# Channel attention and two feed-forward layers on one core: weights in separate tiles, one lag of five, all of layer 2 by Strassen steps, an own order for the end

## The chip, the cores and the metric

One core of a Trainium2 chip runs the whole program. The metric is the device time of one execution in microseconds (us). The kernel before took 1023.1 to 1024.99 us in three runs, with a median of 1024.78 us. The core's engines are PE (matrix products), DVE (vector), ACT (scalar and activation functions), POOL (a second elementwise engine) and SP (which issues the transfers). Each works through its own queue in order.

## The reference

All arrays are float32. There are 6016 tokens, 256 channels and a hidden width of 2048.

```python
qn = q / (np.linalg.norm(q, axis=1, keepdims=True) + 1e-06)     # over the tokens
kn = k / (np.linalg.norm(k, axis=1, keepdims=True) + 1e-06)
s = kn.transpose(0, 2, 1) @ qn / tau                            # 256 x 256
a = softmax(s)                                                  # over the last axis
x = (v @ a)                                                     # 6016 x 256
h = x @ moe_w_in;  x = (h - np.tanh(h)) @ moe_w_out             # 256 -> 2048 -> 256
h = x @ moe2_w_in
g = np.where(h > 0.0, h, np.exp(np.minimum(h, 0.0)) - 1.0)
out = g @ moe2_w_out
```

## The kernel before

**Values in two parts.** A float32 matrix is held as a high part (rounded to what PE multiplies in one pass) and a low part (the rest). A product is three matmuls: high by high, high weights by low values, low weights by high values. `win` and `wout` hold one layer's two weight matrices, high and low part in one tile each.

**Blocks and steps.** After the attention (whose 256 by 256 matrix is folded into layer 1's first weights) the tokens are worked in 12 blocks, 11 of 512 tokens and a last, narrow one of 384. A step (layer, block b, slice p of 0 to 7) makes 256 of the 2048 hidden values for one block: the first products, the activation, the split of the result into `ghi` (ACT, L917) and `glo` (POOL, L920), and 12 matmuls that add its share to the two output sums `o0` and `o1` (PSUM, L1018). The code counts layers from 0: `(0, 11, p)` is layer 1's narrow block and `(1, 0, p)` the first block of layer 2.

**Plain and Strassen steps.** A plain step's first products are 12 matmuls with 512 columns (384 in the narrow block). A Strassen step (`Step.one` to `Step.seventh`) makes seven products of half blocks, 21 matmuls with 256 columns, from sums of the weights (`ws`, loaded from DRAM for every step into three buffers, L666) and of the values (`thi`, `tlo`). Its chain `qa` is read three times on the way by ACT (`copies`, L860); DVE joins the pieces (`merge` L864, `close` L870, `close_chain` L875). In layer 2 before, `strassen` is true for the 512-wide blocks except for slice 5 (`PLAIN`). The sums for layer 2 are made on POOL while layer 1 runs (`sums_of`).

**What sets the order.** Nothing schedules: each engine works in the order in which the code issues. From layer 1's narrow block to the end one loop over `i` (L1235) issues one step per turn and, between its pieces, work of earlier steps: the activation of step i-2, its end and split of step i-3 (`three`; in layer 1 all of it with step i-2), and the output products of an old step. That is step i-4 in layer 1 and step i-5 in layer 2, so that the turn i = 12 has none; turns 0, 1 and 3 carry those of layer 1's last 512-wide block. When an old step has p = 7, its block's sums are complete: `emit_evac` moves `o0` by ACT at the end of the turn and `o1` at the beginning of the next turn (`behind`; ACT in layer 1 except in its last block, otherwise DVE). The next turn's old step has p = 0 and starts the same two sums again (a boundary, `boundary`). In layer 2 this turn is always a step with p = 5. Within a Strassen turn the last two products of the step before (`tail.four`, `tail.three`, issued by `finish`) come after six output products and after `six` and `five`.

**The transition.** While layer 1's narrow block runs, the turns issue on SP the loads of layer 2's weights: `win` slice p after step (0, 11, p) has used the old one (L1386), `wout` slice p after the output products of (0, 11, p) (L1372), 512 KB each, and `ws` two steps ahead.

**The end.** After the last step five turns with no new step remain (`cur is None`). They finish the activations of the last three steps and issue the output products of the last five. `exp` of a step goes into one PSUM tile (`ps_b`, one buffer), so that it waits for the `end` of the step before.

Of the kernel before, what the change touches and what calls it, by code (L numbers as in the profile page):

```python
# [8 lines left out]
F32 = mybir.dt.float32  # L9
# [13 lines left out]
def kernel(  # L23
# [40 lines left out]
    win_hi, win_lo = win[:, 0], win[:, 1]  # L64
    wout_hi, wout_lo = wout[:, 0], wout[:, 1]

    PAIRS = (1, 3, 5, 7)
    PLAIN = (5,)

# [455 lines left out]
    with tc.manual_schedule():  # L525
# [271 lines left out]
        class Step:  # L797
# [87 lines left out]
                else:  # L885
                    nc.vector.tensor_copy(out=self.h[:, 1], in_=q)

            def exp(self):
                self.e = ps_b.tile([P, 2, 512], F32, tag="o", name=f"e{self.name}")[:, :, : self.n]
                nc.scalar.activation(out=self.e, in_=self.h, func=AF.Exp)  # L890

            def tanh(self):
# [339 lines left out]

        halves_of_unit = []
        behind = []
        for i in range(len(todo) + LAG):  # L1235
            cur = None
            if i < len(todo) and todo[i] == (1, 0, 0):
                assert conv.done() and not conv.ready and not sums_left
            if i < len(todo):
                layer, b, p = todo[i]  # L1240
                cur = Step(layer, b, p, sums_at.pop(i, None))
                steps.append(cur)
                if p == 0 and nv < len(phases):
                    load_v(nv)
                    raw_of[0] = v_of[nv]
            prv, two, three = at(i - 1), at(i - 2), at(i - 3)
            tail = prv if prv and prv.seven else None
            old = at(i - 4) if at(i - 4) and at(i - 4).layer == 0 else at(i - 5)
            if old and old.layer == 0 and old is not at(i - 4):
                old = None  # L1250
            parts, done = [], None
            if old:
                done = (old.layer, old.b, old.p)
                parts = out_products(*done, (old.hi, old.lo), last=(i == len(todo) + LAG - 1))
            elif i in early_outs:
                done = early_outs[i][:3]
                parts = out_products(*early_outs[i])
# [4 lines left out]
                    part()  # L1262
                del parts[:n]

            before_act, after_act, scalar_mid, scalar_end, pool_end = [], [], [], [], []
            if cur and nv < len(phases):
# [12 lines left out]
            if cur and layer == 0:  # L1279
# [4 lines left out]
            first = two if two and two.layer == 0 else None  # L1284
            second = two if two and two.layer == 1 else None
            third = three if three and three.layer == 1 else None

            def vector_begin():
                if tail and boundary:
                    tail.merge()  # L1290
                while behind:
                    emit_evac(*behind.pop(), (1,))
                if third:
                    third.end()
                if tail and not boundary:
                    tail.merge()
                for f in before_act:
                    f()
                if first:
                    first.begin()  # L1300

            def finish():
                if tail:
# [7 lines left out]
            def act_b():  # L1311
                if i == 0:
                    before.upper()
                    before.lower()
                if first:
# [6 lines left out]
            if cur is None:  # L1322
                if two:
                    two.tanh()
                vector_begin()
                out(6)
                finish()
            elif cur.seven:
# [6 lines left out]
                out(6)  # L1335
                cur.six()
                cur.copy(2)
                cur.five()
                finish()
            else:  # L1340
                cur.plain(0)
                cur.plain_copy(0)
# [6 lines left out]
                else:  # L1349
                    out(6)  # L1350
                    finish()
            if cur:
                fetch_sums(i + 2)
            act_b()
            if cur is None:
                out(12)
            elif cur.seven:
                out(3)
                cur.seventh()
                cur.copy(1)  # L1360
# [3 lines left out]
                cur.plain_copy(1)  # L1364
                out(12)
            if done:
                last_block = i >= len(todo)
                emit_evac(*done, range(KC) if last_block else (0,))
                if done[2] == NP - 1 and not last_block:
                    behind.append(done)  # L1370
                if done[:2] == (0, NBLK - 1):
                    nc.sync.dma_start(  # L1372
                        out=wout[:, :, 2 * done[2] : 2 * done[2] + 2].bitcast(F32), in_=out_dram2[done[2]]
                    )
            for f in scalar_mid:
                f()
            if third:
                third.upper()
                third.lower(nc.vector if cur is None else None)
            for f in scalar_end:  # L1380
                f()
            for f in pool_end:
                f()
            if cur and (layer, b) == (0, NBLK - 1):
                fs = slice(2 * P * p, 2 * P * (p + 1))
                nc.sync.dma_start(  # L1386
                    out=win[:, :, :, fs].bitcast(F32), in_=in_dram[p].rearrange("p k d i f -> p k d (i f)")
                )
            if cur and p == NP - 1:
                nv += 1  # L1390


# [33 lines left out]
```

## Time and profile before

| | us |
|---|---|
| median of three runs | 1024.78 |
| the profiled execution | 1024.82 |
| its span, first to last instruction | 1023.0 |
| PE busy in the span | 1009.8 |
| DVE, ACT, POOL busy | 816.5, 742.5, 488.2 |

The profile is of one execution. A matmul's busy time is modelled: in a stream one with 512 columns starts about 0.216 us after the last and is shown as 0.38 us long, so starts tell more than lengths. A wait is idle time of an engine, with the instruction whose end released it. The granted clock is a share of 2.4 GHz; 0.5 is 1.2 GHz.

### The profile page before, as it was taken

What the parts mean: (1) busy time and instruction counts of PE and PEld (TensorE: products, weight loads), DVE (VectorE), ACT (ScalarE), POOL (GpSimd) and SP (SyncE); (2) the same over time, 40 slices, a digit from 0 to 9 for tenths busy, and PEclk for the clock granted to TensorE, in tenths of its full rate; (3) what the DMA queues carried; (4) which work ended last, traced back from release to release, by engine and by line L of the source; (5) the groups of instructions that cost most, each with busy time, mean ns of one, the idle gap of its engine ahead of it and who ended that gap; (6) DMA issues with size and microseconds to landing.
All of it is one profiled execution on the core that took longest, in us unless ns stands there. A gap on an engine that the chain in (4) does not pass through costs nothing.

```text
span 1023.0 us, 15755 instructions
## 1 busy us (share of the span) xinstructions
PE 1009.8 (99%) x5935; PEld 922.9 (90%) x5935; DVE 816.5 (80%) x1068; ACT 742.5 (73%) x1086; POOL 488.2 (48%) x309
## 2 busy tenths in 40 slices
PE   9999999999999999999989999999999999999998
PEld 8888888899999999898989999999999999999997
DVE  7899988899999999999536777777777777777765
ACT  7877775656656666576457888888888888888765
POOL 4522210243434342344445676676676666766542
PEclk9999999999999999999999999999999999999999
DMA  9832120232222232221258333433333433333200
GB/s 351 297 103 83 42 93 31 73 103 93 94 72 83 94 112 90 67 94 58 83 185 315 113 104 124 140 108 125 124 124 105 130 135 106 114 119 113 83 9 28
DMA packets 61468, 115.58 MB, mean 113 GB/s; under 512 B 4944, under 2 KB 26704, under 8 KB 61392
## 3 DMA queue, kind: packets, MB, share of 16 engines
q1 hardware_dynamic: 61104, 114.05, 33.1%
q8 instruction: 47, 0.77, 0.3%
q10 hardware_dynamic: 288, 0.52, 0.1%
q14 instruction: 29, 0.24, 0.1%
HBM read 90.18 MB, written 24.38 MB: 112 GB/s over the span
## 4 chain that ended last, share of the span: by engine, by line
PE 95%; DVE 3%; ACT 2%; issue 1%; DVEq 0%; ACTq 0%
PE o L1018 45%; PE h L283 13%; PE qa L830 10%; PE qb L830 7%; PE S L351 4%; PE qb L283 3%; PE qa L283 3%; PE q L756 2%; PE q L755 2%; PE q L754 2%; PE aw L283 1%; PE o_last L1018 1%; DVE g L955 0%; PE warm L363 0%; ACT ghi L917 0%
## 5 line engine op out<-in xcount | busy, mean ns | idle before, releaser
L1018 PE MATMUL o<-ghi,wout 128*128 128x512 f32 (+1 forms) x1472 | 362.3, 378 | 2.7 <-ACT osb L1046 2.7
L920 POOL TENSOR_TENSOR glo<-g,ghi 128x1024 fp32r<-128x1024 f32 (+1 forms) x101 | 233.7, 2314 | 179.8 <-ACT ghi L917 177.1
L1018 PEld LDWEIGHTS o<-ghi,wout 128*128 128x128 f32 x1472 | 262.6, 190 | 29.7 <-ACT osb L1046 3.2
L1018 PE MATMUL o<-glo,wout 128*128 128x512 f32 (+1 forms) x736 | 199.7, 377 | 0.0
L795 POOL TENSOR_TENSOR glo<-g,ghi 128x1024 fp32r<-128x1024 f32 x32 | 76.4, 2386 | 196.7 <-ACT ghi L791 152.0
L902 DVE SCALAR_TENSOR_TENSOR e<-e,g 128x1024 f32<-128x1024 f32 (+1 forms) x96 | 115.8, 1206 | 54.5 <-ACT e L890 54.5
L1018 PEld LDWEIGHTS o<-glo,wout 128*128 128x128 f32 x736 | 133.0, 190 | 15.0
L860 ACT ACTIVATE copies<-qa 128x256 f32<-128x256 f32 x231 | 88.2, 382 | 72.7 <-PE qa L830 72.4
L283 PE MATMUL h<-vhi,win 128*128 128x512 f32 x424 | 134.8, 379 | 0.7 <-DVE g L955 0.7
L910 DVE SCALAR_TENSOR_TENSOR g<-e,hs 128x1024 f32<-128x1024 f32 (+1 forms) x96 | 115.1, 1199 | 6.9 <-DVE e L902 0.5
L917 ACT ACTIVATE ghi<-g 128x1024 fp32r<-128x1024 f32 (+1 forms) x104 | 106.1, 1020 | 7.8 <-DVE g L906 5.4
L895 ACT ACTIVATE g<-hs 128x1024 f32<-128x1024 f32 (+1 forms) x96 | 99.8, 1040 | 0.0
L890 ACT ACTIVATE e<-hs 128x1024 f32<-128x1024 f32 (+1 forms) x96 | 96.9, 1010 | 2.1 <-DVE g L910 2.1
L283 PEld LDWEIGHTS h<-vhi,win 128*128 128x128 f32 x424 | 80.1, 189 | 12.5 <-ACT wout L203 1.1
L783 ACT ACTIVATE g<-hs 128x1024 f32<-128x1024 f32 x32 | 33.9, 1059 | 78.4 <-DVE hs L773 78.4
L791 ACT ACTIVATE ghi<-g 128x1024 fp32r<-128x1024 f32 x64 | 67.6, 1057 | 22.0 <-DVE g L788 22.0
L875 DVE COPY hs<-qa 128x256 f32<-128x256 f32 x77 | 32.5, 423 | 63.9 <-PE qa L830 63.9
L283 PE MATMUL h<-vlo,win 128*128 128x512 f32 x212 | 80.3, 379 | 0.0
L830 PE MATMUL qa<-thi,ws 128*128 128x256 f32 x308 | 76.5, 274 | 1.2 <-ACT copies L860 1.2
L162 DVE CUSTOM_DVE_ANT_0 cut<-cut,low 128x512 uint16<-128x512 uint16 (+1 forms) x48 | 64.6, 1345 | 0.5
L830 PEld LDWEIGHTS qa<-thi,ws 128*128 128x128 f32 x308 | 58.7, 190 | 5.5 <-ACT copies L860 1.4
L864 DVE TENSOR_TENSOR hs<-qb,copies 128x512 f32<-128x512 f32 x77 | 52.4, 680 | 2.0 <-ACT copies L860 2.0
(209 smaller groups left out, 2305.3 us busy)
## 6 DMA issues: line engine op xcount, KB each, us to landing
ws<-sums SPq DMA_DIRECT2D x77, 512.0 KB, 3.3
qk<-in_q_dram SPq DMA_DIRECT2D x23, 256.0 KB, 5.1
vraw<-in_vT_dram SPq DMA_DIRECT2D x11, 512.0 KB, 4.0
x<-osb SPq DMA_DIRECT2D x22, 256.0 KB, 2.0
vraw<-x SPq DMA_DIRECT2D x11, 512.0 KB, 4.3
out_dram<-osb SPq DMA_DIRECT2D x22, 256.0 KB, 2.0
qk<-in_k_dram SPq DMA_DIRECT2D x21, 256.0 KB, 5.2
raw0in<-in_moe_w_in_dram SPq DMA_DIRECT2D x8, 512.0 KB, 3.6
```

The source lines that it names most:

```text
L283: nc.tensor.matmul(out=out, lhsT=w, rhs=x, start=(i == 0), stop=(i == len(pairs) - 1))
L791: nc.scalar.activation(out=self.hi, in_=self.g, func=AF.Copy)
L795: engine.tensor_tensor(out=self.lo, in0=self.g, in1=self.hi.bitcast(F32), op=ALU.subtract)
L830: nc.tensor.matmul(out=out, lhsT=w, rhs=x, start=start and k == 0, stop=k == 2, skip_group_check=True,)
L860: nc.scalar.activation(out=self.copies[:, k], in_=self.qa[:, :W], func=AF.Copy)
L890: nc.scalar.activation(out=self.e, in_=self.h, func=AF.Exp)
L895: nc.scalar.activation(out=self.g, in_=self.h, func=AF.Tanh, scale=0.5)
L902: nc.vector.scalar_tensor_tensor(out=self.e, in0=self.e, scalar=1.0, in1=self.g, op0=ALU.add, op1=ALU.mult)
L910: nc.vector.scalar_tensor_tensor(out=self.g, in0=self.e, scalar=0.0, in1=self.h, op0=ALU.min, op1=ALU.max)
L917: nc.scalar.activation(out=self.hi, in_=self.g, func=AF.Copy)
L920: (engine or nc.gpsimd).tensor_tensor(out=self.lo, in0=self.g, in1=self.hi.bitcast(F32), op=ALU.subtract)
L1018: nc.tensor.matmul(out=columns(o[c][:, :n]), lhsT=w[:, f, c * P : (c + 1) * P], rhs=turned(x[:, i]), start=(f == 0 and w is wout_hi and x ...
```

## The change

1. `win` and `wout` become two tiles each, for the high and the low parts, and each load of layer 2's weights becomes two of 256 KB.
2. `PLAIN` is empty: slice 5 of layer 2's 512-wide blocks becomes a Strassen step too. Its weight sums are made, stored and loaded like the others'. At a boundary a Strassen turn calls `finish` before the six output products.
3. The old step is i-5 in both layers. Layer 1's narrow block splits its activation with step i-3, and turn 12 has output products while turn 4 has none. `o1` of layer 1's last 512-wide block is moved by DVE.
4. The five turns at the end are replaced by a straight list for the last three steps x, y and z; z's `exp` gets a PSUM tile of its own.

```diff
-    win = wpool.tile([P, 2, KC, F], F32R, name="win")
-    wout = wpool.tile([P, 2, F // P, C], F32R, name="wout")
...
+    win_hi, win_lo = win = [wpool.tile([P, KC, F], F32R, name=f"win_{k}") for k in ("hi", "lo")]
+    wout_hi, wout_lo = wout = [wpool.tile([P, F // P, C], F32R, name=f"wout_{k}") for k in ("hi", "lo")]
...
-    PLAIN = (5,)
+    PLAIN = ()
...
-                if c and (layer or b == NBLK - 1):
+                if c and (layer or b >= NBLK - 2):
                     nc.vector.tensor_copy(out=to, in_=of)
...
-            old = at(i - 4) if at(i - 4) and at(i - 4).layer == 0 else at(i - 5)
-            if old and old.layer == 0 and old is not at(i - 4):
-                old = None
+            old = at(i - LAG)
...
-                if first:
-                    first.upper()
-                    first.lower()
-                if second:
-                    second.exp()
-                    second.begin()
+                if two:
+                    two.exp()
+                    two.begin()
...
-                out(6)
-                cur.six()
-                cur.copy(2)
-                cur.five()
-                finish()
+                if boundary:
+                    finish()
+                    out(6)
+                    cur.six()
+                    cur.copy(2)
+                    cur.five()
+                else:
+                    out(6)
+                    cur.six()
+                    cur.copy(2)
+                    cur.five()
+                    finish()
...
+                for k in range(2):
+                    nc.sync.dma_start(
+                        out=win[k][:, :, fs].bitcast(F32), in_=in_dram[p][:, k].rearrange("p d i f -> p d (i f)")
+                    )
...
+        x, y, z = steps[-3:]
+        emit_rest(steps[-5])
+        y.tanh()
+        x.end()
+        x.upper()
+        x.lower()
+        y.exp()
+        y.begin()
+        z.tanh()
+        z.exp(ps_e)
+        emit_rest(steps[-4])
+        y.end()
+        z.begin()
+        y.upper()
+        y.lower()
+        z.end()
+        z.upper()
+        z.lower(nc.vector)
+        emit_rest(x)
+        emit_rest(y)
+        emit_rest(z, last=True)
+        emit_evac(z.layer, z.b, z.p)
```

PE in layer 1's narrow block, before: `qa_11_4` and `qb_11_4` are the two halves of step (0, 11, 4), and `o_0_11` are the two sums of this block.

```order
2392 L283 MATMUL qa_11_4_5282<-vlo_4962,win 128x384
2395 L283 MATMUL qa_11_4_5282<-vhi_4909,win 128x384 x2
2396 L1018 MATMUL o_0_11_5284<-ghi,wout 128x384
2397 L1018 MATMUL o_0_11_5285<-ghi,wout 128x384
2402 L283 MATMUL qb_11_4_5283<-vhi_4909,win 128x384
2406 L283 MATMUL qb_11_4_5283<-vhi_4909,win 128x384 x2
2413 L283 MATMUL qa_11_5_5326<-vhi_4909,win 128x384
```

The same place now:

```order
2492 L281 MATMUL qa_11_4_5293<-vhi_4920,win_hi 128x384
2494 L281 MATMUL qa_11_4_5293<-vhi_4920,win_lo 128x384 x2
2495 L281 MATMUL qb_11_4_5294<-vhi_4920,win_hi 128x384
2499 L281 MATMUL qb_11_4_5294<-vhi_4920,win_lo 128x384 x2
2500 L281 MATMUL qa_11_5_5323<-vhi_4920,win_hi 128x384
2504 L281 MATMUL qa_11_5_5323<-vhi_4920,win_lo 128x384 x2
2505 L1018 MATMUL o_0_11_5325<-ghi,wout_hi 128x384
2506 L1018 MATMUL o_0_11_5326<-ghi,wout_hi 128x384
```

The first output product of the narrow block has moved from the middle of step 4 to the middle of step 5, behind the second half of step 4 and the first of step 5.

PE at a boundary of layer 2, before: the end of turn (1, 1, 4), then turn (1, 1, 5); `o_1_0` are the sums of block 0, `o_1_1` those of block 1.

```order
2878 L1018 MATMUL o_1_0_5724<-glo,wout 128x512
2879 L283 MATMUL qa_1_5_6167<-vhi_5556,win 128x512
2880 L283 MATMUL qa_1_5_6167<-vlo_5558,win 128x512
2881 L283 MATMUL qa_1_5_6167<-vhi_5556,win 128x512
2882 L283 MATMUL qa_1_5_6167<-vlo_5558,win 128x512
2883 L283 MATMUL qa_1_5_6167<-vhi_5556,win 128x512 x2
2884 L830 MATMUL qa_1_4_6105<-thi_5717,win 128x256
2889 L830 MATMUL qb_1_4_6106<-vhi_5556,ws_6030 128x256
```

The same place now:

```order
2988 L1018 MATMUL o_1_0_5751<-glo,wout_hi 128x512
2989 L828 MATMUL qa_1_5_6212<-vhi_5563,win_hi 128x256
2991 L828 MATMUL qa_1_5_6212<-vhi_5563,win_lo 128x256
2992 L828 MATMUL qb_1_5_6213<-vhi_5563,win_hi 128x256
2994 L828 MATMUL qb_1_5_6213<-vhi_5563,win_lo 128x256
2995 L828 MATMUL qa_1_4_6150<-thi_5743,win_hi 128x256
3000 L828 MATMUL qb_1_4_6151<-vhi_5563,ws_6073 128x256
3001 L1018 MATMUL o_1_1_6215<-ghi,wout_hi 128x512
```

Between the last product of the old sums and the first of the new stand 12 matmuls with 256 columns; before, there were six with 512 columns and six with 256.

ACT in the last stretch, before, from the `hs` of the last step on (`g` is `tanh`, `e_11_6` and `e_11_7` the `exp` of the last two steps, `ghi` the split):

```order
1054 L884 ACTIVATE hs<-qa_11_7_10650 128x384
1055 L895 ACTIVATE g<-hs 128x2x384
1056 L890 ACTIVATE e_11_5_10669<-hs 128x2x384
1057 L917 ACTIVATE ghi<-g 128x2x384
1058 L895 ACTIVATE g<-hs 128x2x384
1059 L890 ACTIVATE e_11_6_10698<-hs 128x2x384
1060 L917 ACTIVATE ghi<-g 128x2x384
1061 L895 ACTIVATE g<-hs 128x2x384
1062 L890 ACTIVATE e_11_7_10720<-hs 128x2x384
1063 L917 ACTIVATE ghi<-g 128x2x384 x2
```

The same stretch now:

```order
1074 L882 ACTIVATE hs<-qa_11_7_10853 128x384
1075 L895 ACTIVATE g<-hs 128x2x384
1076 L890 ACTIVATE e_11_5_10872<-hs 128x2x384
1077 L917 ACTIVATE ghi<-g 128x2x384
1078 L895 ACTIVATE g<-hs 128x2x384
1079 L917 ACTIVATE ghi<-g 128x2x384
1080 L890 ACTIVATE e_11_6_10915<-hs 128x2x384
1081 L895 ACTIVATE g<-hs 128x2x384
1082 L890 ACTIVATE e_11_7_10920<-hs 128x2x384
1083 L917 ACTIVATE ghi<-g 128x2x384 x2
```

The split of step x stands before the `exp` of step y instead of behind it.

## Rows read from the trace of the kernel before

**Rows 1.** Windows, from:to, length, busy by engine, PE clock, DMA share, GB/s.

```profile
510.00:560.00 50.00, 46.10 (x292) 44.58 (x292) 23.91 (x36) 32.38 (x53) 24.48 (x16) 0.97 0.67 235
600.00:975.00 375.00, 375.00 (x2402) 347.65 (x2401) 278.05 (x368) 310.86 (x480) 247.33 (x138) 1.00 0.35 117
975.00:1023.00 48.00, 43.01 (x242) 40.21 (x240) 27.59 (x35) 27.67 (x39) 16.66 (x9) 1.00 0.05 20
```

**Rows 2.** Waits of PE: who waited for whom, us in total, times, longest.

```profile
PE o L1018 <- ACT osb L1046: 2.7, 2, 1.5
PE o_last L1018 <- ACT ghi L917: 1.5, 2, 0.8
PE qa L830 <- ACT copies L860: 1.2, 1, 1.2
PE qb L830 <- DVE hs L864: 0.3, 1, 0.3
```

**Rows 3.** Timeline, narrow block: start, us, engine, instruction, idle before.

```profile
518.09 0.33 PE L283 MATMUL qa<-vhi,win 128*128 128x384 f32 x1
...
519.28 1.01 ACT L1046 ACTIVATE osb<-o 128x512 f32<-128x512 f32 x1
...
522.31 1.79 PE L1018 MATMUL o<-ghi,wout 128*128 128x384 f32 x5 [1.54 <-ACT osb L1046]
...
526.86 0.33 PE L283 MATMUL qa<-vhi,win 128*128 128x384 f32 x1
...
530.76 0.33 PE L283 MATMUL qa<-vhi,win 128*128 128x384 f32 x1
```

**Rows 4.** Windows, PE alone: length, PE busy, granted clock, DMA.

```profile
521.00:524.00 3.00, 1.69 (x6) 0.76 0.80 261
```

**Rows 5.** Chain of waits, in order of time: first six output products of three turns.

```profile
595.41 1.30 PE o L1018 x6
...
610.46 1.30 PE o L1018 x6
615.39 1.30 PE o L1018 x6
```

**Rows 6.** Timeline, all engines, boundary turn (1, 1, 5).

```profile
599.51 0.38 PE L283 MATMUL qa<-vhi,win 128*128 128x512 f32 x1
599.55 0.68 DVE L864 TENSOR_TENSOR hs<-qb,copies 128x512 f32<-128x512 f32 x1
...
600.15 0.68 DVE L1044 COPY osb<-o 128x512 f32<-128x512 f32 x1
...
600.75 1.21 DVE L910 SCALAR_TENSOR_TENSOR g<-e,hs 128x1024 f32<-128x1024 f32 x1
600.80 0.27 PE L830 MATMUL qa<-thi,win 128*128 128x256 f32 x1
...
601.47 1.46 PE L1018 MATMUL o<-ghi,wout 128*128 128x512 f32 x6
```

**Rows 7.** Windows, start of layer 2.

```profile
535.00:555.00 20.00, 20.00 (x148) 19.80 (x148) 10.40 (x16) 14.68 (x27) 11.05 (x7) 1.00 0.95 353
```

**Rows 8.** DMA, window 540.55:541: issue, count, KB each, us to landing.

```profile
ws<-sums SPq DMA_DIRECT2D x1, 512.0 KB, 7.5
```

**Rows 9.** Timeline, PE: the first product that reads these sums.

```profile
548.22 0.35 PE L830 MATMUL qa<-thi,ws 128*128 128x256 f32 x1
```

**Rows 10.** Timeline, all engines, the end of the program.

```profile
1007.29 1.46 PE L1018 MATMUL o_last<-ghi,wout 128*128 128x384 f32 x8
1007.39 1.83 POOL L920 TENSOR_TENSOR glo<-g,ghi 128x768 fp32r<-128x768 f32 x1 [2.08 <-ACT ghi L917]
...
1007.92 0.95 DVE L910 SCALAR_TENSOR_TENSOR g<-e,hs 128x768 f32<-128x768 f32 x1
1008.90 0.81 ACT L890 ACTIVATE e<-hs 128x768 f32<-128x768 f32 x1 [0.86 <-DVE g L910]
...
1019.07 0.49 PE L1018 MATMUL o_last<-glo,wout 128*128 128x384 f32 x2
```

More of the change, by code (lines that the diff above doesn't have):

```diff
@@ L886, in plain_copy, with exp @@
                     nc.vector.tensor_copy(out=self.h[:, 1], in_=q)
-            def exp(self):
-                self.e = ps_b.tile([P, 2, 512], F32, tag="o", name=f"e{self.name}")[:, :, : self.n]
+            def exp(self, pool=None):
+                if self.layer == 0:
+                    return
+                self.e = (pool or ps_b).tile([P, 2, 512], F32, tag="o", name=f"e{self.name}")[:, :, : self.n]
                 nc.scalar.activation(out=self.e, in_=self.h, func=AF.Exp)
@@ L1234 @@
         behind = []
-        for i in range(len(todo) + LAG):
-            cur = None
-            if i < len(todo) and todo[i] == (1, 0, 0):
+        for i in range(len(todo)):
+            layer, b, p = todo[i]
+            if todo[i] == (1, 0, 0):
                 assert conv.done() and not conv.ready and not sums_left
[L1239 to L1245, printed above, removed]
+            cur = Step(layer, b, p, sums_at.pop(i, None))
+            steps.append(cur)
+            if p == 0 and nv < len(phases):
+                load_v(nv)
+                raw_of[0] = v_of[nv]
             prv, two, three = at(i - 1), at(i - 2), at(i - 3)
             tail = prv if prv and prv.seven else None
-            old = at(i - 4) if at(i - 4) and at(i - 4).layer == 0 else at(i - 5)
-            if old and old.layer == 0 and old is not at(i - 4):
-                old = None
+            old = at(i - LAG)
             parts, done = [], None
@@ L1253 @@
                 done = (old.layer, old.b, old.p)
-                parts = out_products(*done, (old.hi, old.lo), last=(i == len(todo) + LAG - 1))
+                parts = out_products(*done, (old.hi, old.lo))
             elif i in early_outs:
@@ L1278 @@
                     pool_end.append(lambda: half_of_sums_lower(nv, p - 5))
-            if cur and layer == 0:
+            if layer == 0:
                 vector, scalar, pool = conversion(i)
@@ L1283 @@
                 pool_end += pool
-            first = two if two and two.layer == 0 else None
-            second = two if two and two.layer == 1 else None
-            third = three if three and three.layer == 1 else None
             def vector_begin():
@@ L1292, in vector_begin @@
                     emit_evac(*behind.pop(), (1,))
-                if third:
-                    third.end()
+                if three:
+                    three.end()
                 if tail and not boundary:
@@ L1314, in act_b @@
                     before.lower()
[L1315 to L1328 removed]
+                if two:
+                    two.exp()
+                    two.begin()
+            if cur.seven:
                 cur.one()
@@ L1351 @@
                     finish()
-            if cur:
-                fetch_sums(i + 2)
+            fetch_sums(i + 2)
             act_b()
-            if cur is None:
-                out(12)
-            elif cur.seven:
+            if cur.seven:
                 out(3)
@@ L1366 @@
             if done:
-                last_block = i >= len(todo)
-                emit_evac(*done, range(KC) if last_block else (0,))
-                if done[2] == NP - 1 and not last_block:
+                emit_evac(*done, (0,))
+                if done[2] == NP - 1:
                     behind.append(done)
                 if done[:2] == (0, NBLK - 1):
[L1372 to L1379, printed above, removed]
+                    for k in range(2):
+                        nc.sync.dma_start(
+                            out=wout[k][:, 2 * done[2] : 2 * done[2] + 2].bitcast(F32),
+                            in_=out_dram2[done[2]][:, k],
+                        )
+            if three:
+                three.upper()
+                three.lower()
             for f in scalar_end:
@@ L1383, with emit_rest @@
                 f()
-            if cur and (layer, b) == (0, NBLK - 1):
+            if (layer, b) == (0, NBLK - 1):
                 fs = slice(2 * P * p, 2 * P * (p + 1))
[L1386 to L1389, printed above, removed]
-                nv += 1
+                for k in range(2):
+                    nc.sync.dma_start(
+                        out=win[k][:, :, fs].bitcast(F32), in_=in_dram[p][:, k].rearrange("p d i f -> p d (i f)")
+                    )
+            if p == NP - 1:
+                nv += 1
+        h_stack.close()
+        ps_e = h_stack.enter_context(tc.tile_pool(name="ps_e", bufs=1, space=PSUM, side="right"))
+        def emit_rest(step, last=False):
+            for part in out_products(step.layer, step.b, step.p, (step.hi, step.lo), last=last):
+                part()
+        x, y, z = steps[-3:]
[20 more added lines that the diff above has]
+        emit_evac(z.layer, z.b, z.p)
 def kernel(**inputs):
```

9 lines of the change are left out of this document (2 added, 7 removed).

## The prediction

> **What bounds the kernel now.** PE does. I read the page's busy times first (PE 1009.8 of 1023.0 us, the others at most 816.5), then the windows by stage, the waits of PE, and the timeline where a wait ends. In the long middle of layer 2 PE is busy for 375.00 of 375.00 us, so there only PE work can be saved. PE has holes in two places: 3.90 us of the 50 us in which layer 1's narrow block gives way to layer 2, and 4.99 us of the last 48 [rows 1]. The waits name what ends the holes: the moving of the output sums by ACT (2.7 us), the split of the last steps (1.5 us), one wait for a copy (1.2) and one for a merge (0.3) [rows 2]. The change touches exactly the steady middle and these holes.
>
> The profiled execution took 1024.82 us, of which 1.82 lie outside its span; the median of the runs is 1024.78. The sum below is made against 1024.8.
>
> **A. The lag of five in the narrow block.** Turn 4 begins at 518.09 and turn 5 at 526.86: 8.77 us. The next turn, with the same 24 matmuls of 384 columns, takes 526.86 to 530.76: 3.90 us, or 0.163 per matmul. So turn 4 loses 4.87 us [rows 3]. In it PE waits twice for ACT, which moves both sums of the block before. Behind the waits the granted clock is 0.76 over a stretch in which its two levels are 2.4 and 1.2 GHz, so part of it ran at 1.2 GHz after PE had stood still [rows 4]. Now turn 4 has no output products; the first of the narrow block come after two half steps more, 1.96 us of PE work later, and DVE takes one of the two sums while ACT takes the other. ACT's first move starts at 519.28 and takes 1.01 [rows 3], so with DVE on the other sum both are free at about 520.3; the new place is reached at 518.09 + 3 x 0.98 = 521.0. The stall goes, and the drop of the clock with it. Gain 4.87; ends 0 (if another wait stands in turns 4 to 6) and 4.87. I take 4.87: the sums are free 0.7 us before they are wanted, and with the moves halved ACT has caught up by then.
>
> **B. The turn 12 gets output products.** Its `six` now has six matmuls of 384 columns (0.98 us) before it, so the wait of 1.2 us for `copies` goes; the wait of 0.3 for a merge belongs to the same place [rows 2]. An idle is counted from the modelled end of a matmul, 0.27 after its start, where the next would have started after 0.11, so each of the two hides 0.16 more: 1.2 + 0.3 + 0.3 = 1.8. Against it stand two new costs. The first boundary of layer 2 has the moves of layer 1's sums in front of it, 1.01 long where DVE's move in layer 2 takes 0.68 [rows 3, 6]: 0.3. And the loads: from 535 to 555 the transfers are busy 0.95 of the time [rows 7]; the `ws` issued in the window from 540.55 took 7.5 us, so it landed after 548.05, and the product that reads it started at 548.22, just behind [rows 8, 9]. With A the readers come 4.9 us earlier. The issues come earlier too, because they hang on PE's turns, and one `wout` load fewer stands ahead of each `ws`; but SP issues two transfers for each one. I count 0.5, between 0 (they keep pace) and 2.5 (half of A is lost to the loads). Net 1.0.
>
> **C. Slice 5 by Strassen.** In the chain the same point of two neighbouring Strassen turns is 615.39 - 610.46 = 4.93 apart; the three turns around a plain step take 610.46 - 595.41 = 15.05, where three Strassen turns would take 14.80 [rows 5]. Difference 0.25, and by matmuls: 12 at 0.215 (six from 599.51 to 600.80) against 21 at 0.112 (six from 600.80 to 601.47) [rows 6] is 2.58 against 2.35, 0.23. So 0.25 for each of the 11 blocks: 2.75. The sums for slice 5 add five POOL instructions, one cast on ACT and one transfer in layer 1, beside PE's work as the seven others do; ACT gets two copies more per block and DVE two short instructions more, in turns in which both have room: over the middle they are busy 0.83 and 0.74 [rows 1].
>
> What can take it back is the boundary. Between the old and the new sums stood 601.47 - 599.51 = 1.96 us of PE work; now it is 12 x 0.112 = 1.34. DVE merges (599.55), then moves `o1` from 600.15 to 600.83, which is 1.32 after the turn's begin [rows 6]; the second output product would start at 1.34 + 0.22, with its weights loaded from 1.34 on. So it fits with nothing to spare. `three` needs the merge's end, 600.23, that is 0.72, and comes at 1.0. I take 0.03 per boundary from these rows, 0.3 in all; ends 0 and 0.25 per boundary (a late wait and a restart). Net 2.5, ends 0 and 2.75.
>
> For this step the Trainium skill ("TensorE: Matmul & The Clock Gate", section on the back-to-back issue gap) speaks against the change: it gives a sustained rate of about 81 ns per matmul with 128 columns and 131 with 512, so that cost would go more by the number of matmuls than by columns. With an estimate of 98 ns for 256 from that page, 21 cost 2.06 and 12 cost 1.57: 0.49 dearer per block. The trace has 215 and 112 ns [rows 6], which is the same section's figure for an isolated matmul. It is the third rival.
>
> **D. The end.** Five steps' output products remain from 1007.29 on, 60 at 0.163: 9.8. The last two start at 1019.07, so the last is through at 1019.40 and 2.3 us were lost [rows 10]. In the new order, with 0.81 for an ACT instruction, 0.95 for DVE's and 1.83 for POOL's: x ends on DVE at 1008.87, its split is made by ACT at 1009.7 (before, ACT did y's `exp` first), POOL is through at 1011.6. y: `exp` 1010.5, DVE 1011.45 and 1012.35, ACT 1013.2, POOL 1015.05. z: DVE 1013.2 and 1014.05, ACT 1014.9, DVE 1015.9. PE: three steps until 1013.14, y's eight first products until 1014.5, wait for POOL until 1015.1, four more until 1015.8, and z, whose parts are ready, until 1017.75. Gain 1.65. What is late now is y's low part, since POOL is twice as slow as DVE was. Ends 0.6 (each step on ACT and DVE 0.1 later) and 2.3.
>
> The separate tiles remove no wait that ends late in the rows, and I count them at nothing beside what stands in B: SP has room, and if its issues were late, it is the first rival that follows.
>
> **The sum.** 4.87 + 1.0 + 2.5 + 1.65 = 10.0; 1024.8 - 10.0 = 1014.8.
>
> **Rivals.** First: the loads cannot follow. For it speaks that they are at 0.95 and that one product already starts behind its load [rows 7 to 9]; against it, that each load's issue moves with PE's turns and that one `wout` less stands ahead. Then B's 0.5 becomes 2.5 to 4, and the time is 1016.8 to 1018.3.
>
> Second: the boundary is late by 0.25 at each of the 11. For it, that the rows leave nothing to spare there; against it, that DVE's instructions stand in the same place at each boundary, so that 0.03 is what they say. C becomes 0: 1017.3.
>
> Third: the price goes by matmuls. A Strassen step then costs the plain step's 2.58 and nine spacings of 0.112 more, C is a loss of 11 x 9 x 0.112 = 11.1, and the time 1024.8 - 7.5 + 11.1 = 1028.4. Against it: layer 2 already has 77 such turns, seven in each of 11 blocks, and two neighbours stand 4.93 apart, less than a plain turn [rows 5].
>
> Fourth, on the other side: at the boundary DVE gets an instruction of 1.21 (`L910`, which now stands behind the move of `o1`) between the merge and the move, or ACT's copies slip behind it, so that PE stands for more than 1 us at each. The gains besides C are 7.5, so it is slower from (7.5 + 2.75) / 11 = 0.93 per boundary on; at 1.21 [rows 6] the time would be 1024.8 - 7.5 - 2.75 + 13.3 = 1027.9. Against it: the order on DVE puts the move first, and a wait of that length would need ACT or DVE to be short of time over a whole turn, which the middle does not show [rows 1].
>
> Fifth: the stall of turn 4 only moves, to turn 5 or to turn 8, and A gives 1 instead of 4.87: 1018.7.
>
> **Chances.** Forecast 0.62; loads 0.16; late boundary 0.09; A only moved 0.06; slower by the boundary 0.03; by matmuls 0.01; all terms at their upper ends (4.87 + 1.8 + 2.75 + 2.3 = 11.7, 1013.1) 0.03. The range takes in the loads and the late boundary above; below it goes to 1011.9, the upper ends less the 1.2 by which a median of three may differ between runs that spread over 1.9: 1011.9 to 1018.3. A difference under 0.2% (2 us) cannot be told from none. Faster 0.95, same 0.02, slower 0.03.
>
> **What would show it.** A: no wait of PE for `osb` in layer 1's narrow block, its clock at 1.0 throughout, turn 4 at 1.96 us. B: turn 12 without a wait for `copies`; if the loads are late, PE waits for `ws` or ACT for `vraw` in the third turn of layer 2. C: eight turns of 4.93 in each block, 39.5 us, and less than 0.1 at each boundary. D: PE's last product about 1.6 us nearer to its ideal, with one wait for POOL in step y. I am wrong if PE still idles 3 us in the transition, if the boundaries show a wait of 0.2 or more, or if a new wait stands in layer 1's long part, where POOL's added sums lie.

## The result and the profile after

The changed kernel took 1015.49 us (median of five, 1014.83 to 1015.76) against 1023.2 of the kernel before (five runs, 1023.0 to 1024.99): ratio 0.9917, 95% interval 0.9903 to 0.9932. In a later comparison it took 1015.31 against 1024.64 of 15 runs, ratio 0.9912 [0.9894, 0.9930]. The forecast was 1014.8 in a range of 1011.9 to 1018.3. Profiled run against profiled run it is 1014.89 against 1024.82: 9.9 us less, and the span is 10.6 us less (1012.4 against 1023.0), where the sum said 10.0.

First the windows of the changed kernel, with the columns of [rows 1], [rows 4] and [rows 7]; the second and third end 10.6 us earlier than in [rows 1], as the program does, and the fourth is of PE alone.

```profile
510.00:560.00 50.00, 50.00 (x333) 48.42 (x332) 32.47 (x43) 36.76 (x62) 30.32 (x20) 1.00 0.78 271
600.00:964.40 364.40, 364.40 (x2437) 341.04 (x2436) 280.00 (x380) 303.98 (x488) 241.07 (x135) 1.00 0.38 130
964.40:1012.40 48.00, 44.06 (x250) 41.45 (x248) 26.54 (x34) 28.96 (x41) 21.61 (x11) 1.00 0.05 20
...
521.00:524.00 3.00, 3.00 (x20) 1.00 0.84 216
...
535.00:555.00 20.00, 20.00 (x150) 19.30 (x150) 14.26 (x21) 16.83 (x30) 11.95 (x8) 1.00 0.87 318
```

The transition is full: 50.00 of 50.00 where PE had 46.10 [rows 1], and at 521 to 524 the clock is 1.00 where it was 0.76 [rows 4]. The window from 535 to 555 holds later work than in [rows 7], since the third turn of layer 2 now comes about 7 us earlier (541.3 against 548.2); its 0.87 is therefore no relief. In the window from 528 to 548, which holds about the same work, the transfers are at 0.97, where they were at 0.95. At the end 3.94 us of idle are left of 4.99 [rows 1].

The waits of PE from 500 us on, which answer to [rows 2]:

```profile
PE o_last L1018 <- POOL glo L920: 0.3, 1, 0.3
PE o_last L1018 <- ACT ghi L917: 0.3, 1, 0.3
```

The waits for `osb`, `copies` and `hs` are gone; of 1.5 us for `ghi` 0.3 is left, and one of 0.3 for `glo` is new. The last two output products start at 1008.56, 10.51 us earlier than in [rows 10]. The narrow block, all engines, start and length in us, answers to [rows 3]:

```profile
518.04 1.05 ACT L1046 ACTIVATE osb<-o 128x512 f32<-128x512 f32 x1 [2.15 <-PE o L1018]
518.05 0.33 PE L281 MATMUL qa<-vhi,win_hi 128*128 128x384 f32 x1
...
518.25 1.05 DVE L1044 COPY osb<-o 128x512 f32<-128x512 f32 x1 [0.74 <-PE o L1018]
...
520.00 0.33 PE L281 MATMUL qa<-vhi,win_hi 128*128 128x384 f32 x1
...
520.98 0.49 PE L1018 MATMUL o<-ghi,wout_hi 128*128 128x384 f32 x2
```

Turn 4 runs from 518.05 to 520.00, 1.95 us where the prediction asked for 1.96. The two moves stand beside each other and end by 519.30; PE wants the sums at 520.98, so 1.7 us are to spare. ACT started its move at once here, since with the lag of five the split of an earlier step stands behind it (518.89). In the kernel before the split stood in front, and itself waited for DVE:

```profile
518.53 0.84 ACT L917 ACTIVATE ghi<-g 128x768 fp32r<-128x768 f32 x1 [1.02 <-DVE g L906]
```

A boundary between two wide blocks, all engines, answers to [rows 6]:

```profile
592.68 0.27 PE L828 MATMUL qa<-vhi,win_hi 128*128 128x256 f32 x1
592.72 0.68 DVE L862 TENSOR_TENSOR hs<-qb,copies 128x512 f32<-128x512 f32 x1
...
593.32 0.68 DVE L1044 COPY osb<-o 128x512 f32<-128x512 f32 x1
...
593.92 1.21 DVE L910 SCALAR_TENSOR_TENSOR g<-e,hs 128x1024 f32<-128x1024 f32 x1
594.01 1.03 PE L1018 MATMUL o<-ghi,wout_hi 128*128 128x512 f32 x4
```

DVE's move of `o1` ends 1.32 us after the turn's begin, and the four output products follow from 1.33 on without a gap in between. The instruction of 1.21 us stands behind the move, not in front of it.

### The profile page after: what moved, and what is told of

Its sections match the earlier page's. It is cut to its first block, busy times and chain, and to the rows that moved or that the text cites. A ratio compares the mean times of both kernels' runs of the same rounds, so it can differ in the third digit from the quotient of the medians.

```text
span 1012.4 us, 16071 instructions
## 1 busy us (share of the span) xinstructions
PE 1004.4 (99%) x6034; PEld 922.2 (91%) x6034; DVE 826.9 (82%) x1089; ACT 742.3 (73%) x1108; POOL 495.6 (49%) x316
## 4 chain that ended last, share of the span: by engine, by line
PE 96%; DVE 2%; issue 1%; ACT 0%; POOL 0%; POOLq 0%; DVEq 0%; ACTq 0%
PE o L1018 46%; PE h L281 13%; PE qa L828 12%; PE qb L828 9%; PE S L349 4%; PE q L753 2%; PE q L754 2%; PE q L752 2%; PE qa L281 2%; PE qb L281 1%; PE aw L281 1%; PE o_last L1018 1%; DVE g L955 0%; PE warm L361 0%; DVE glo L950 0%
## 5 line engine op out<-in xcount | busy, mean ns | idle before, releaser
L1018 PE MATMUL o<-ghi,wout_lo 128*128 128x512 f32 (+1 forms) x736 | 203.6, 377 | 0.0
L1018 PE MATMUL o<-glo,wout_hi 128*128 128x512 f32 (+1 forms) x736 | 201.8, 377 | 0.0
L1018 PE MATMUL o<-ghi,wout_hi 128*128 128x512 f32 (+1 forms) x736 | 187.7, 377 | 0.0
L858 ACT ACTIVATE copies<-qa 128x256 f32<-128x256 f32 x264 | 100.6, 381 | 71.8 <-PE qa L828 71.6
L1018 PEld LDWEIGHTS o<-glo,wout_hi 128*128 128x128 f32 x736 | 132.2, 190 | 14.4
L1018 PEld LDWEIGHTS o<-ghi,wout_lo 128*128 128x128 f32 x736 | 132.1, 190 | 14.0
L1018 PEld LDWEIGHTS o<-ghi,wout_hi 128*128 128x128 f32 x736 | 129.4, 190 | 11.8 <-DVE osb L1044 0.2
L890 ACT ACTIVATE e<-hs 128x1024 f32<-128x1024 f32 (+1 forms) x96 | 97.0, 1010 | 0.0
L828 PE MATMUL qa<-thi,ws 128*128 128x256 f32 x352 | 87.5, 274 | 0.0
L281 PE MATMUL h<-vhi,win_hi 128*128 128x512 f32 x212 | 80.4, 379 | 0.7 <-DVE g L955 0.7
L281 PE MATMUL h<-vlo,win_hi 128*128 128x512 f32 x212 | 80.3, 379 | 0.0
```

The lines of the kernel that those rows point to most:

```text
L281: nc.tensor.matmul(out=out, lhsT=w, rhs=x, start=(i == 0), stop=(i == len(pairs) - 1))
L828: nc.tensor.matmul(out=out, lhsT=w, rhs=x, start=start and k == 0, stop=k == 2, skip_group_check=True,)
L858: nc.scalar.activation(out=self.copies[:, k], in_=self.qa[:, :W], func=AF.Copy)
L1018: nc.tensor.matmul(out=columns(o[c][:, :n]), lhsT=w[:, f, c * P : (c + 1) * P], rhs=turned(x[:, i]), start=(f == 0 and w is wout_hi and x ...
```

## The experiments

All but the last are edits of the changed kernel or that kernel itself; its nine runs have a median of 1015.4 (1014.8 to 1016.6), and medians are set against that; a term's size is read from the traces, where it stands in one place. "Gap" is the time by which two matmuls start further apart than in a full stream (0.216 us for 512 columns, 0.163 for 384, 0.111 for 256).

**undo_c: slice 5 plain again** (part C).

```diff
-    PLAIN = ()
+    PLAIN = (5,)
```

> The changed kernel (1015.5, median of five) with slice 5 computed plainly again in layer 2's eleven wide blocks. Theory (price by columns, 0.25 us per block, no cost at the boundaries): 2.5 to 2.75 us slower, 1018.0 to 1018.3, and the stretch of the eleven blocks longer by the same amount. Rival, boundary late by 0.25 in the changed kernel: no difference, 1015.5. Rival, price by the number of matmuls: 11 us faster, about 1004.5.

Measured: 1017.18 (1016.14 to 1017.6). Two neighbouring moves of `o1` by DVE, first of this kernel, then of the changed one:

```profile
593.58 0.68 DVE L1044 COPY osb<-o 128x512 f32<-128x512 f32 x1
...
633.30 0.68 DVE L1044 COPY osb<-o 128x512 f32<-128x512 f32 x1
```

```profile
632.80 0.68 DVE L1044 COPY osb<-o 128x512 f32<-128x512 f32 x1
```

With 593.32 from above the changed kernel takes 39.48 us per block, this one 39.72: 0.24 to 0.25 for each block, eight turns of 4.935, where [rows 5] had 4.93. Eleven blocks make 2.7 us. The runs are 1.8 us apart, with spreads of 1.5 to 1.8 in each. A part of the difference stands at the first boundary of layer 2 (551 to 600 us): the changed kernel has gaps of 0.40 us there, this one, whose turn there is plain, 0.03. So slice 5 by Strassen steps gains 2.7 in the blocks and costs 0.4 at the first boundary, 2.3 net. With fewer matmuls the kernel is slower, not 11 us faster: the price goes by columns. The sustained rate of the Trainium skill ("TensorE: Matmul & The Clock Gate", section on the back-to-back issue gap), some 131 ns at 512 columns and 81 at 128, would have made it faster, by the prediction's estimate from it; this trace, at 216 and 111 ns for 512 and 256, disagrees.

**boundary_old_order: output products before `four` and `three` at a boundary too.**

```diff
-                if boundary:
-                    finish()
-                    out(6)
-                    cur.six()
...
-                else:
-                    out(6)
...
+                out(6)
+                cur.six()
+                cur.copy(2)
+                cur.five()
+                finish()
```

> The changed kernel with the Strassen turn's usual order also in the first turn of a block: output products right after one and two, before four and three of the step before. Theory (the changed order is what hides DVE's move of o1, which ends 1.3 us after the turn's begin, while the second output product would now come at 0.9): a wait of 0.4 to 0.7 us with its restart at each of 11 boundaries, 4.5 to 7.5 us slower, 1020 to 1023, and PE waits for DVE's osb 11 times. Rival, DVE's move runs early enough in either order: no difference, 1015.5.

Measured: 1021.33 (1020.22 to 1023.36), 5.9 slower. PE's wait, and one boundary (all engines):

```profile
PE o L1018 <- DVE osb L1044: 3.0, 11, 0.4
```

```profile
595.08 0.27 PE L828 MATMUL qa<-vhi,win_hi 128*128 128x256 f32 x1
...
595.72 0.68 DVE L1044 COPY osb<-o 128x512 f32<-128x512 f32 x1
595.74 0.45 PE L1018 MATMUL o<-ghi,wout_hi 128*128 128x512 f32 x1
...
596.45 0.92 PE L1018 MATMUL o<-ghi,wout_hi 128*128 128x512 f32 x3 [0.25 <-DVE osb L1044]
```

The move ends 1.32 us after the turn's begin as before, but PE comes for the second sum at 0.88 (0.216 after 595.74), 0.67 earlier than in the new order (1.33 + 0.216), by the six matmuls that stood in front. There is a gap of 0.49 and one of 0.10 behind it at each of ten boundaries, 0.6 us, though the wait reads 0.25; the first boundary loses more. So the gain of C hangs on the new order: without it the boundaries would cost more than twice what C gains.

**undo_ab: the old lag in the narrow block** (parts A and B).

```diff
-            old = at(i - LAG)
+            old = at(i - 4) if at(i - 4) and at(i - 4).layer == 0 else at(i - 5)
+            if old and old.layer == 0 and old is not at(i - 4):
+                old = None
...
-                if c and (layer or b >= NBLK - 2):
+                if c and (layer or b == NBLK - 1):
...
```

Not shown of this edit: layer 1's activation is ended and split with step i-2 again, as in the kernel before.

> The changed kernel with the old lag in layer 1's narrow block (output products four turns behind, no output products in turn 12, both sums moved by ACT), all else as changed. Theory: 5.9 us slower (4.9 of turn 4 and 1.0 of turn 12), 1021.4; PE waits for osb 2.7 us and for copies 1.2 us; a stretch behind the osb wait at the lower clock in some runs but not in all, so that the runs fall into two groups about 1.7 us apart (mean clock 0.998 in the one, 1.0 in the other), as those of the kernel before do. Rival, the stall is given back later because the loads of layer 2 bound this stretch: 1 to 3 us slower, 1016.5 to 1018.5. Rival for the two groups: the clock is not it, and both kinds of run show the same clock.

Measured: 1021.93 (1020.51 to 1023.71), 6.5 slower. PE's waits:

```profile
PE o L1018 <- ACT osb L1046: 2.7, 2, 1.5
PE qa L828 <- ACT copies L858: 1.2, 1, 1.2
PE qb L828 <- DVE hs L862: 0.9, 1, 0.9
PE qa L828 <- DMA ws<-sums: 0.7, 1, 0.7
```

Its gaps are 4.9 us in turn 4, 1.5 at turn 12's `copies`, 1.3 around the wait for `hs` (the first boundary, now a Strassen turn) and 0.9 more for `ws` than the changed kernel's profile had. The twelve runs lie at 1020.5 to 1020.8, 1021.5 to 1022.6 and 1023.6 to 1023.7. The mean granted clock of a run is 1.000 in the three runs at 1020.51, 1020.71 and 1020.75, and 0.996 to 0.998 in the nine others, all of which took longer. So the clock does part the runs, as the expectation said; among the nine a second cause spreads the times.

**lag_four_dve_moves: the same, but DVE moves the second sum** (undo_ab without the last two lines shown).

> The kernel undo_ab (old lag of four, turn 12 without output products), but DVE moves the second sum. Theory: of the stall of 4.8 us in turn 4 the first wait remains (ACT's move ends at 520.3, PE wants it at 519.1: 1.3 us and a restart), the second goes; 1.3 to 1.5 us lost there if the clock stays at 1.0, 3 us if it drops as behind the two waits: 1018.5 or 1020 against 1021.9. Rival, the length of the waits doesn't matter and the second is only longer or moved: 1021.9.

Measured: 1019.74 (1019.38 to 1020.99), 2.2 less than undo_ab. Windows of PE alone (length, busy, granted clock, DMA), first of undo_ab, then of this kernel:

```profile
518.00:521.00 3.00, 1.39 (x7) 1.00 0.04 14
521.00:524.00 3.00, 1.94 (x9) 0.84 0.83 246
524.00:527.00 3.00, 3.00 (x13) 0.59 0.24 89
```

```profile
518.00:521.00 3.00, 1.87 (x12) 1.00 0.13 48
521.00:524.00 3.00, 3.00 (x21) 1.00 0.72 203
524.00:527.00 3.00, 3.00 (x20) 1.00 0.96 283
```

One gap of 1.3 us is left, the clock stays at 2.4 GHz, and turn 4 loses 1.4 instead of 4.9. Of the 3.5 us between them the second gap is half (1.8); the rest are some eleven matmuls that start 0.32 apart instead of 0.163, the rate at 1.2 GHz. All five runs have a mean clock of 0.999 or 1.000.

**lag_five_act_moves: the lag of five, but ACT moves both sums.**

```diff
-                if c and (layer or b >= NBLK - 2):
+                if c and (layer or b == NBLK - 1):
```

> The changed kernel with the lag of five, but both sums of layer 1's block 10 moved by ACT. Theory: ACT gets the second move behind the copy and the tanh of turn 4, that is from about 520.8 to 521.8; PE wants that sum at 521.2, so it waits once for ACT's osb, 0.6 us and a restart of 0.1: 0.7 us slower, 1016.1, the clock stays at 1.0. Rival, the lag alone hides both moves: no difference, 1015.4. Rival, ACT falls behind for several turns: 2 us or more slower.

Measured: 1016.47 (1015.56 to 1017.5), 1.1 slower. All engines:

```profile
520.37 1.06 ACT L1046 ACTIVATE osb<-o 128x512 f32<-128x512 f32 x1
...
520.63 0.33 PE L1018 MATMUL o<-ghi,wout_hi 128*128 128x384 f32 x1
...
521.49 0.76 PE L1018 MATMUL o<-ghi,wout_hi 128*128 128x384 f32 x3 [0.53 <-ACT osb L1046]
```

The gap is 0.70 and 0.10 behind it. The lag hides the first move, and DVE's help the second. Turn 4 loses 4.9 us with neither, 1.4 with the helper alone, 0.8 with the lag alone and nothing with both. So either part by itself takes most of the stall, because either leaves a single gap and the clock at 2.4 GHz; the last 0.8 or 1.4 needs both.

**undo_d: the old end.** The last five turns run in the loop again, `exp`, split and products in its rhythm, and the lines from `x, y, z = steps[-3:]` on are gone.

> The changed kernel with the old order of the last five turns (each turn tanh, merge, exp, split in the rhythm of the loop). Theory of the prediction: 1.65 us slower, 1017.1. By the trace of the changed kernel, where PE still loses 1.1 us at the end against 2.3 before: 1.2 us slower, 1016.7. Rival, the end is set by the last move and store whatever PE does: no difference, 1015.5.

Measured: 1016.06 (1015.88 to 1017.12), 0.7 slower. PE's wait:

```profile
PE o_last L1018 <- ACT ghi L917: 1.5, 2, 0.8
```

PE's gaps at the end are 2.49 us, as in the kernel before, against 1.26 in the changed one: D is worth 1.23.

**one_tile: `win` and `wout` in one tile each, one load for both parts.**

```diff
-    win_hi, win_lo = win = [wpool.tile([P, KC, F], F32R, name=f"win_{k}") for k in ("hi", "lo")]
...
+    win = wpool.tile([P, 2, KC, F], F32R, name="win")
...
+    win_hi, win_lo = win[:, 0], win[:, 1]
...
-                    for k in range(2):
-                        nc.sync.dma_start(
...
+                    nc.sync.dma_start(
...
```

> The changed kernel with high and low parts of win and of wout in one tile each again, and one load for both instead of two. Theory of the prediction (no wait that ends late hangs on it): no difference, 1015.2 to 1015.8. Rival, the loads cannot follow the faster transition unless each part has its own tile and load: PE waits for weights at the beginning of layer 2, 0.5 to 3 us slower, 1016.0 to 1018.5.

Measured: 1014.68 (1014.5 to 1014.92); its ratio to the kernel before is 0.9907 [0.9891, 0.9923], where the changed kernel has 0.9912 and 0.9917. The separate tiles win nothing. Its profile has the gaps of the changed kernel, 0.9 us in front of the third `ws` among them. Whether the separate tiles cost up to 0.7 us stays open, since the two kernels were not run side by side.

**changed_again: the changed kernel once more.**

> The changed kernel again, beside the next three on one chip. Theory: its runs spread because the load of the third ws of layer 2 lands at or up to 1.3 us after the point where PE wants it: 1014.5 to 1016.0, and the PE gap between 535 and 551 us of the profiled run is what its span has above 1012.2. Rival: the spread comes from the beginning (before 100 us), and that gap is the same 0.2 us.

Measured: 1015.31 (1015.08 to 1016.57), span 1013.4. PE, in front of the third `ws`:

```profile
541.26 0.49 PE L1018 MATMUL o<-ghi,wout_lo 128*128 128x384 f32 x2
542.31 0.35 PE L828 MATMUL qa<-thi,ws 128*128 128x256 f32 x1 [0.56 <-DMA ws<-sums]
```

In the first profile this product came just behind its load:

```profile
541.32 0.35 PE L828 MATMUL qa<-thi,ws 128*128 128x256 f32 x1
```

Its gaps there were 0.05 and 0.08; here it waits, and the gaps from 535 to 551 us are 1.1 instead of 0.25. That is 0.9 of the 1.0 us between the two spans. In the experiments that keep the order of the loads it was 0.5 (undo_d) to 1.7 (boundary_old_order), so that the first profile has the least of all. The kernel before has the same race: its load took 7.5 us and the product came just behind it [rows 8, 9].

**sums_three_ahead: the first three `ws` a turn earlier.**

```diff
-            fetch_sums(i + 2)
+            if i + 3 <= NP + 2:
+                fetch_sums(i + 3)
+            elif i + 2 > NP + 2:
+                fetch_sums(i + 2)
```

> The changed kernel with the first three ws loads of layer 2 issued one turn earlier (their buffers are free), so each stands ahead of one more turn's win and wout loads in SP's queue. Theory (that load bounds the transition in most runs): PE has no gap for ws at 541 us, 0.2 to 1.3 us less, 1014.3 with a spread under 0.8. Rival, the queue is bound by volume and the wait passes to win, wout or vraw: no difference, 1015.5. Rival, the spread is not from there: no difference.

Measured: 1014.31 (1013.78 to 1015.27), 1.1 less than the changed kernel. The wait for `ws` is gone, but not all of the gap: 0.6 is left, against 1.1 in changed_again, so the traces show half of the gain in this place and the rest is not accounted for. All engines:

```profile
540.51 0.63 ACT L697 ACTIVATE vhi<-vraw 128x512 fp32r<-128x512 f32 x1 [0.28 <-DMA vraw<-x]
...
541.05 0.37 ACT L858 ACTIVATE copies<-qa 128x256 f32<-128x256 f32 x1
...
541.47 0.38 PE L828 MATMUL qa<-thi,ws 128*128 128x256 f32 x1 [0.25 <-ACT copies L858]
```

Now ACT waits for `vraw`, the copy behind it on ACT is late, and PE with it: the next link of the same shortage, as this run's first rival had it. The prediction had named both signs, PE's wait for `ws` and ACT's for `vraw`.

**end_y_exp_first: y's `exp` ahead of x's split, into a buffer of its own.**

```diff
-        ps_e = h_stack.enter_context(tc.tile_pool(name="ps_e", bufs=1, space=PSUM, side="right"))
+        ps_e = h_stack.enter_context(tc.tile_pool(name="ps_e", bufs=2, space=PSUM, side="right"))
...
+        y.exp(ps_e)
         x.end()
         x.upper()
         x.lower()
-        y.exp()
         y.begin()
```

> The changed kernel with y's exp ahead of x's split on ACT, into a buffer of its own. In the changed kernel ACT idles 0.92 us before x's split and y's begin waits 1.67 us on DVE for that exp. Theory: y's chain is 1.2 us earlier, PE's two waits at the end (0.26 for ghi, 0.34 for glo, 1.1 us with their restarts) go: 1.1 us faster, 1014.4, with the last pair of output products at 1007.5 against 1008.6 and the gap at the end below 0.2 us. Rival, z's split becomes late in place of y's: 0 to 0.4 us.

Measured: 1014.53 (1013.88 to 1014.88), 0.9 less. First the changed kernel's end, then this one's, rows of all engines:

```profile
999.68 0.84 ACT L917 ACTIVATE ghi<-g 128x768 fp32r<-128x768 f32 x1 [0.92 <-DVE g L910]
1000.43 0.80 ACT L890 ACTIVATE e<-hs 128x768 f32<-128x768 f32 x1
...
1001.26 0.97 DVE L902 SCALAR_TENSOR_TENSOR e<-e,g 128x768 f32<-128x768 f32 x1 [1.67 <-ACT e L890]
...
1003.38 0.84 ACT L917 ACTIVATE ghi<-g 128x768 fp32r<-128x768 f32 x1 [0.69 <-DVE g L910]
...
1004.28 0.92 PE L1018 MATMUL o_last<-ghi,wout_hi 128*128 128x384 f32 x4 [0.26 <-ACT ghi L917]
...
1006.18 0.92 PE L1018 MATMUL o_last<-glo,wout_hi 128*128 128x384 f32 x4 [0.34 <-POOL glo L920]
```

```profile
999.23 0.82 ACT L890 ACTIVATE e<-hs 128x768 f32<-128x768 f32 x1
...
1000.08 0.97 DVE L902 SCALAR_TENSOR_TENSOR e<-e,g 128x768 f32<-128x768 f32 x1
...
1004.27 0.81 PE L1018 MATMUL o_last<-ghi,wout_hi 128*128 128x384 f32 x4
```

The `exp` fills what were 0.92 us of idle on ACT, DVE goes on at once, and PE's gaps at the end fall from 1.26 to 0.14. The last pair of output products starts at 1007.85 instead of the 1007.5 that was expected, since this run also lost 1.0 in front of the third `ws`.

**both_mends: the last two together.**

> The changed kernel with y's exp first at the end and the first three ws loads a turn earlier. Theory, the two add up: 1.1 us at the end and 0.5 to 1.0 in front of layer 2's third turn, 1013.3 to 1013.9. Rival, one hides the other: 1014.3.

Measured: 1013.96 (1013.69 to 1014.01), ratio to the kernel before 0.9896 [0.9883, 0.9910]: 1.4 us less than the changed kernel, and the best version here. In the medians that is less than the sum of the two, 2.0. In the traces they add up: the gaps are 0.6 in front of the third `ws` and 0.14 at the end, as with each edit alone.

**before_again: the kernel before once more.**

> The kernel before, once more with a profile. Theory on the spread of its runs (1022.5 to 1027.2): the time above 1022.5 is the load gap of PE between 535 and 560 us (0.2 to 1.7 us, varying) and the stretch at the lower clock behind the osb wait, so the two profiles of before differ by what these two differ. Rival, the difference lies in the first 100 us or is not in PE's gaps at all.

Measured: 1025.21, span 1023.4. Windows of PE alone:

```profile
521.00:524.00 3.00, 1.95 (x6) 0.64 0.87 279
524.00:527.00 3.00, 3.00 (x17) 0.79 0.15 56
```

Its gaps are 4.75 us in turn 4, 0.93 at 535 to 551 us (0.17 in the first profile) and 2.20 up to 600 us, as before. The load gap moves by 0.8, as it does from run to run of the changed kernel. The low clock is in all three profiles that have both waits for `osb`; in each the mean clock is 0.998, and no other stretch between 0 and 1010 us is below 1.00. Such runs are not all of them. Of 41 runs of the kernel before whose mean clock is known it is 1.000 in 19, at 1022.5 to 1024.3 us with a median of 1023.25, and 0.996 to 0.998 in 22, at 1024.2 to 1027.2 with a median of 1025.35. So the times part at the clock, almost without overlap, and the medians are 2.1 us apart; the doubled spacings of the profile account for 1.7. That the runs at 1.000 have the same waits is not shown, since none of the profiles is of such a run.

## Why the prediction was right, point by point

The gaps of PE in the two first profiles and the block spacing give the ledger. It closes to 0.1: 10.5 us of PE time, 10.6 us of span.

| term | gap before | gap after | gain | predicted |
|---|---|---|---|---|
| A, turn 4 | 4.86 | 0.00 | 4.9 | 4.87 |
| B, turn 12 and first boundary (551 to 600 us) | 2.19 | 0.40 | 1.8 | 1.5 |
| B, loads (535 to 551 us) | 0.17 | 0.25 | -0.1 | -0.5 |
| C, 11 blocks at 0.25 | | | 2.7 | 2.5 |
| D, the end | 2.49 | 1.26 | 1.2 | 1.65 |

In the sum B (1.7 instead of 1.0) and D (1.2 instead of 1.65) miss in opposite directions and partly cancel.

**A** came out as said, and by the said mechanism: the lag and the second mover each hide one move, and the full clock comes back with the stall gone. "A only moved" is out: no wait stands in turns 4 to 8. But 4.87 is the price in a run whose clock drops behind the waits. Less the 1.7 us of doubled spacings it is about 3.2, an estimate for the runs of the kernel before with a mean clock of 1.000. The prediction took one profile for all runs here.

**B** was a little too low. The holes of turn 12 and the boundary were 2.19 from start to start, not 1.8, since three more gaps of 0.10 stand behind them. These are their two rows in the kernel before, with gaps of 1.41 and 0.48:

```profile
557.31 0.38 PE L830 MATMUL qa<-thi,ws 128*128 128x256 f32 x1 [1.24 <-ACT copies L860]
...
561.31 0.38 PE L830 MATMUL qb<-vhi,ws 128*128 128x256 f32 x1 [0.32 <-DVE hs L864]
```

The price at the first boundary (0.3) was 0.40, a late `hs` and `o1`, as DVE's move took 0.84 there, in the changed kernel:

```profile
553.76 0.84 DVE L1044 COPY osb<-o 128x384 f32<-128x384 f32 x1
```

By undo_c this is a price of C, which the prediction booked under B. The 0.5 for the loads was 0.1 in the first profile and 0.9 in the second: not a constant, but a race that each run ends differently. That it is nearly nothing in the ledger is luck, as the first profile has the least load gap of all that keep this order. The bounds of 0 and 2.5 held; the step that read one landing time from one profile had no way to see that.

**C**: 39.48 us per block against the 39.5 forecast. The ten boundaries between wide blocks cost nothing at all instead of 0.03, since the move of `o1` ends where the rows of before put it (1.32), and the output products came at 1.33. The second rival and the fourth fail on that row, the third on undo_c. That little was to spare there is shown by boundary_old_order, where coming 0.67 us earlier costs 0.49 and a restart of 0.10; by these numbers about 0.2 was.

**D** is the term that was mis-sized: 1.65 against 1.23. The order and the wait for POOL were as said, but the hand-overs between ACT and DVE took 0.03 to 0.1 us each, which the sum left out, and the instructions up to 0.03 more, so y's split ended at 1004.22 instead of 1003.9 (the predicted times less the 9.3 us by which x's end moved). That opened a second wait of PE, for ACT's `ghi`, with a restart, and brought POOL in later. The prediction had such delays in its lower end (0.6) and put none into the value it took.

**The times.** The sum was made against a profiled run with the low clock, which stands in the upper half of the runs of before (1022.5 to 1027.2, median 1024.4 of 46). The gain was 7.7 us by the first medians, 9.3 by the later ones, 9.0 by all runs; against the 19 runs of before with a mean clock of 1.000 it is 7.9, against the other 22 it is 10.0. The first median of five (1023.2) gave a smaller gain than the sum, and three of those five lie at 1023.0 to 1023.2, where in the later runs the clock is 1.000. The forecast of the changed kernel's time, 1014.8, missed its nine runs' median by 0.6: D's 0.4 and the loads up, B and C down, and the rest is time outside the span, which was 1.8 us before and 1.8 to 2.7 in the changed kernel.

## What to carry to other kernels

Count a stall from start to start, not by the wait in the list: waits of 0.25 and 0.53 us cost 0.6 and 0.8, and two waits of 2.7 in all cost 4.9 where a clock drop followed. When a step gets shorter on the engine that bounds, lay out who must be done before its next consumer, and reorder the independent products into that place: the 0.67 us of products moved there saved 0.6 us at each boundary, more than twice the 0.25 that the shorter step wins. Where one load lands within 0.2 us of its use in a profile, give it a range and not a price: here other runs waited up to 0.9 us. Before a gain is taken from one profile, see whether that run is like the others: here its mean clock is 0.998, nearly half of the runs have 1.000, and part of the stall is not in those.

## What the runs showed that was not expected

A gap of 1.3 us left the granted clock at 2.4 GHz (lag_four_dve_moves), while gaps of 1.3 and 1.8 us with a single matmul between them were followed by some 10 matmuls at 1.2 GHz in each of three profiles. By the mean clocks the drop does not come in every run: 22 of 41 of the kernel before and 9 of 12 of undo_ab are below 0.999. What decides it is not shown.

The wait for loads is one chain: with `ws` in time, ACT stood for `vraw`, and PE for the copy behind it.
